# The first stage of an inverse transform, four steps at once on TensorE tiles of 32 by 64, in a kernel of one spectral and two token layers

## Chip, cores and metric

The kernel runs on one core of a Trainium2 chip. The metric is the device time of one execution in microseconds (us), as the median of three runs. Traces come from one profiled execution.

## What is computed

The input `x` is 8 batches of 3072 rows of 256 columns in f32. A spectral layer is followed by two token layers, which see all 24576 rows. Only the first is touched by the change:

```python
X = np.fft.rfft(x, axis=1)
Yr = Xr @ w_r - Xi @ w_i + b_r
Yi = Xr @ w_i + Xi @ w_r + b_i
Yr = np.sign(Yr) * np.maximum(np.abs(Yr) - lam, 0.0)      # Yi alike, lam = 0.01
y = np.fft.irfft(Yr + 1j * Yi, n=3072, axis=1)
# then per token: h = y @ w_in; (h - tanh(h)) @ w_out; soft mixture of 8 experts
```

## The kernel before

The work is a spectral phase and a token phase. Both are written as generators: a step of the one is issued, then pieces of the other where `TOKENS_BESIDE` (line 44) says so. Each engine takes its instructions in the order in which they are written out; there is no planner in the spectral phase.

The transform of 3072 points is split in two stages of small matrices each way. The forward first stage (`f1_piece`, eight pieces a batch, matmuls at line 253) multiplies by `c1` on tiles of 48 rows and 64 columns, two row groups and two column groups, and goes through DRAM (`ad`) to change the layout. Then a batch is worked off in 12 steps of one pair of frequency groups each (`NP` = 12, loop at line 564, 96 steps and 12 more to drain):

- `f2_pair`: eight matmul instructions (line 289) for the second forward stage, evicted by ScalarE (298, 300) and split in a high and a low part (VectorE 301 and 312, `split_sum` on ScalarE 319 and GpSimd 320);
- `mix_part` for the pair before (line 330): `pa` (6 instructions) and `pmix` (12; 18 for the last pair of a batch), 256 columns each; `add_bias` (VectorE 360) reads `pa` from its one PSUM bank, `shrink` (371, 372) adds `pmix`, clips to plus and minus `LAM`, and subtracts the clipped part (380): four pieces of 64 partitions, two on VectorE and two on GpSimd, which also bring the data into the layout that i1 wants;
- `i1_pair` for the pair before that (line 387): one f32 matmul with a 128 x 128 table and 512 columns, which the trace shows as two passes, evicted by ScalarE (389); its store to DRAM (`vd`) is issued at the start of the next step (`flush`);
- `i2_half` (line 415): the second stage of the inverse for the batch before, 16 halves a batch. In the steady state steps 5 to 7 of a batch and steps 0 to 4 of the next take one each, steps 8 to 11 two each. For the last two batches it is two a step; for the last one of all they stand alone after step 96 + 3. ScalarE evicts to `yt` (422; for the last batch 422 and 426), which is stored to `yd`, where the token phase reads it;
- `f1_piece` of the next batch in steps 0 to 7, one each;
- narrowing of f64 weights that the token phase needs, nine small VectorE instructions (lines 496 to 502) per block of 256 columns, one block every three steps, loaded as `raw` one step ahead of use; folding of some of them on TensorE (465, 478).

PSUM has eight banks. Before, `psl` has two for i2 (`i2`, one of them shared with f1) and one for i1; `ps` has two for `pmix`, one each for f1, `f2` and `pa`. The token phase takes over five of them when the spectral steps are over (`ctx.close` at step 96), and the rest later.

All loads and stores named here are issued from SyncE's queue (SP), in the order of the code: flushed stores, then loads of `x` and `v`, stores of `yd`, loads of `a2` and at last `raw`.

In the token phase the lines to know are 748 (plain matmuls of the first chunk), 831 (GpSimd's subtraction of 128 x 512), 894 (logits, `logit_mm`, on four tiles of 128 rows and 32 columns) and 657 (`low_y`).

Of the kernel before, what the change touches and what calls it, by code (L numbers as in the profile page):

```python
# [43 lines left out]
TOKENS_BESIDE = {-4: 1, -2: 1, 0: 1, 1: 2, 2: 3, 3: 4}  # L44


def dft_tables():
# [71 lines left out]
    for j in range(16):  # L119
# [7 lines left out]
    i2[95, : N2 * N1] = (2.0 / S) * np.cos(np.pi * (nn // 32))  # L127
    return {
        "c1": c1.reshape(128, 64).astype(np.float32),
        "f2": f2.reshape(128, NG * 128).astype(np.float32),  # L130
        "i1": i1.reshape(128, 256).astype(np.float32),
        "i2": i2.astype(np.float32),
# [3 lines left out]
def spectral_phase(tc, nb, x, w_r, w_i, b_r, b_i, tb, yd, w_in, w_out, phi, ident, wo32, wh, wl, wp, ew):  # L136

    nc = tc.nc
    with ExitStack() as late, ExitStack() as mid, ExitStack() as ctx:
# [12 lines left out]
        ps = ctx.enter_context(tc.tile_pool(name="fps", bufs=2, space=PSUM))  # L152
# [55 lines left out]
        def load_mix():  # L208
            for w in (w_r, w_i):
                t = thp.tile([128, 512], F32, tag="sw", name="wst", bufs=3)  # L210
# [29 lines left out]
        def f1_piece(b, i):  # L240
            if b == 0 and i < 6:
                asb = stage[i // 3][:, 2 * (i % 3):2 * (i % 3) + 2]
            else:
                asb = ew.gp.tile([128, 2, 512], F32, tag=f"g{3 + i % 2}", name="asb")
            x = xt.pop((b, i))
            tags = ("i2", "f1") if b else (("mix", "f1"), ("mix", "f2"))[i % 2]
            p = [
                psl.tile([128, 512], F32, tag=t, name="pf1") if t == "i2" else
                ps.tile([128, 512], F32, tag=t, name="pf1", bufs=2 if t == "mix" else 1) for t in tags
            ]  # L250
            for c in range(2):
# [5 lines left out]
            for r in range(2):  # L257
                if b == 0 and r == 1 and i not in ACT_F1:
                    nc.vector.tensor_copy(asb[:, r], p[r])
                else:  # L260
                    nc.scalar.activation(asb[:, r], p[r], AF.Copy)
# [70 lines left out]
        def mix_part(b, i, r):  # L332
# [34 lines left out]
        def shrink(b, i):  # L367
# [6 lines left out]
            v = sh[b, i] = thp.tile([128, 2, 256], F32, tag="sw", name="sw", bufs=3)  # L374
            for gg in range(2):
                q = slice(64 * gg, 64 * gg + 64)
                for ri in (1 - gg, gg):
                    e = slice(256 * ri, 256 * ri + 256)
                    eng = nc.gpsimd if ri == gg else nc.vector
                    eng.tensor_tensor(out=v[64 * ri:64 * ri + 64, gg], in0=t[q, e], in1=c[q, e], op=ALU.subtract)  # L380

        def i1_pair(b, i):
            t = sh.pop((b, i)).rearrange("p g e -> p (g e)")
            p = psl.tile([128, 512], F32, tag="i1", name="pi1", bufs=1)
            last = i == NP - 1
# [6 lines left out]
            stores.append((vd[b].rearrange("(g k) (n d) -> (k n) g d", k=4, n=N2)[:, 2 * i:2 * i + 2, :], vs))  # L392
# [125 lines left out]
        if True:  # L518
            load_f2(0, 2)
            for i in range(8):  # L520
                f1_piece(0, i)
# [12 lines left out]
            load_x(1, 2)  # L534
# [3 lines left out]
            for k in range(1, nb):  # L538
                for j in range(8):
                    pieces_at[NP * (k - 1) + j] = (k, j)  # L540

            def piece(t):
                return [pieces_at[t]] if t in pieces_at else []
# [20 lines left out]
            for s in range(T + NP):  # L564
# [15 lines left out]
                if not due:  # L580
                    for j in piece(s):
                        f1_piece(*j)
# [7 lines left out]
                if due:  # L590
                    for j in piece(s):
                        f1_piece(*j)
# [10 lines left out]
                if 2 <= s <= T + 1:  # L603
                    i1_pair(*divmod(s - 2, NP))
# [17 lines left out]
def token_phase(tc, nch, yd, wh, wl, wp, ident, ew):  # L622
# [9 lines left out]
    with ExitStack() as ctx:  # L632
# [21 lines left out]
        def low_y(c):  # L654
            hi, t = ys[c]
            eng = nc.vector if c == 1 else nc.gpsimd
# [60 lines left out]
        def bank(owner=None):  # L717
# [8 lines left out]
            return (ps if k < 4 else ps2).tile([128, 512], F32, tag=f"b{k}", name="ph")  # L726
# [160 lines left out]
        def logit_mm(c, p):  # L887

            if p == 0:
                lp[c] = ps.tile([128, 512], F32, tag="l", name="pl", bufs=1)  # L890
# [143 lines left out]
        ps2 = None  # L1034
# [511 lines left out]
```

## Time and profile before

| | before |
|---|---|
| median of 3 runs | 2079.85 us |
| lowest, highest | 2078.04, 2084.21 us |
| the profiled execution's own time | 2082.89 us |
| span of its trace | 2081.1 us |
| TensorE busy | 1985.7 us (95%) |
| VectorE busy | 1816.1 us (87%) |
| ScalarE busy | 1315.9 us (63%) |
| GpSimd busy | 1348.7 us (65%) |
| granted TensorE clock, mean | 0.980 |

The busy time of TensorE is modelled, since its matmuls are pipelined; durations of single matmuls therefore overlap, and their spacing tells more than their length. The spectral phase fills the first third of the span. Within it, times are best read by batch, that is from the first `f2_pair` matmul of one batch to that of the next, and within a batch by the chain of waits, which lists what followed what on the engine that was late.

### The profile page before, as it was taken

The page shows a single profiled execution, that of the slowest core. Times are in us where ns is not written, and L with a number is a line of the kernel's source. Part 1 is how long each engine was busy: PE and PEld are TensorE (multiplying, and loading weights), DVE is VectorE, ACT ScalarE, POOL GpSimd, SP SyncE. Part 2 cuts the span into 40 slices and gives each one's busy share as a digit, 9 for nine tenths or more (in the row PEclk, how much of TensorE's full clock was granted, in tenths as well). Part 3 has the DMA queues.
Part 4 walks back from the last instruction along what each step waited for, and adds up shares of the span by engine and source line. Part 5 has one row for each costly group of instructions (what it writes and reads, how often), then busy time and mean ns, then how long its engine had stood idle before and what let it go on. Part 6 is the DMA issues. An engine that isn't in the chain of part 4 may idle for free.

```text
span 2081.1 us, 51288 instructions
## 1 busy us (share of the span) xinstructions
PE 1985.7 (95%) x19214; PEld 1683.4 (81%) x19214; DVE 1816.1 (87%) x3555; ACT 1315.9 (63%) x2528; POOL 1348.7 (65%) x1214
## 2 busy tenths in 40 slices
PE   4899999999999999999999999999999999999875
PEld 2678878877887888888888888888888888888633
DVE  3999889999997799999999999999999999999645
ACT  2456666666555666666767666667666676676424
POOL 0444434444442988888888888888888888888300
PEclk7999999999999999999999999999999999999996
DMA  9788898898665677777777777777777777777899
GB/s 268 231 249 262 273 303 261 275 287 268 222 211 182 151 179 175 176 182 175 180 184 178 176 184 173 181 177 180 179 176 181 178 178 183 178 176 183 250 370 385
DMA packets 250550, 445.46 MB, mean 214 GB/s; under 512 B 36160, under 2 KB 144448, under 8 KB 250048
## 3 DMA queue, kind: packets, MB, share of 16 engines
q1 hardware_dynamic: 249264, 440.59, 77.8%
q8 instruction: 153, 2.51, 0.5%
q10 hardware_dynamic: 1040, 1.61, 0.2%
q14 instruction: 93, 0.76, 0.1%
HBM read 139.01 MB, written 105.91 MB: 118 GB/s over the span
## 4 chain that ended last, share of the span: by engine, by line
PE 78%; DVE 12%; DMA 6%; issue 2%; ACT 1%; SPq 1%; POOL 0%; DVEq 0%; ACTq 0%
PE ph L778 45%; PE pl L894 8%; PE pd L1014 8%; PE pmix L330 3%; PE pi L415 3%; DVE sw L380 3%; PE pf L289 2%; PE pi L387 2%; PE pa L330 2%; PE pf L253 2%; DVE t L371 2%; DVE xml L301 1%; DVE t L360 1%; DMA out_dram<-gq 1%; PE ph L748 1%
## 5 line engine op out<-in xcount | busy, mean ns | idle before, releaser
L831 POOL TENSOR_TENSOR g<-g,tanh 128x512 f32<-128x512 f32 x558 | 710.0, 1300 | 159.5 <-ACT tanh L819 159.4
L843 DVE STREAM_TRANSPOSE gt<-g 128x512 f32<-128x512 f32 x752 | 479.1, 680 | 0.5 <-POOL wl L708 0.3
L789 ACT ACTIVATE g<-ph 128x512 f32<-128x512 f32 x564 | 333.1, 591 | 226.8 <-PE ph L778 217.8
L778 PE MATMUL ph<-th,s 128*128 128x256 f32 x2256 | 456.5, 285 | 0.7 <-ACT g L789 0.7
L804 DVE TENSOR_TENSOR g<-ph,g 128x512 f32<-128x512 f32 x564 | 372.8, 681 | 69.0 <-ACT g L789 35.1
L819 ACT ACTIVATE tanh<-g 128x512 f32<-128x512 f32 x564 | 336.9, 621 | 102.6 <-DVE g L804 66.0
L778 PEld LDWEIGHTS ph<-th,s 128*128 128x128 f32 x2256 | 369.9, 191 | 20.2 <-issue 19.4
L778 PE MATMUL ph<-tl,s 128*128 128x256 f32 x1128 | 318.8, 283 | 0.0
L778 PE MATMUL ph<-yh,wl 128*128 128x256 f32 x1128 | 315.9, 280 | 0.0
L778 PE MATMUL ph<-yh,wh 128*128 128x256 f32 x1128 | 315.2, 279 | 0.0
L778 PE MATMUL ph<-y,wh 128*128 128x256 f32 x1128 | 315.1, 279 | 0.0
L380 POOL TENSOR_TENSOR sw<-t,c 64x256 f32<-64x256 f32 x192 | 169.9, 885 | 165.4 <-DVE c L372 121.7
L778 PEld LDWEIGHTS ph<-tl,s 128*128 128x128 f32 x1128 | 215.1, 191 | 0.0
L778 PEld LDWEIGHTS ph<-yh,wh 128*128 128x128 f32 x1128 | 212.9, 189 | 0.1
L778 PEld LDWEIGHTS ph<-y,wh 128*128 128x128 f32 x1128 | 212.1, 188 | 0.0
L778 PEld LDWEIGHTS ph<-yh,wl 128*128 128x128 f32 x1128 | 212.0, 188 | 0.0
L320 POOL TENSOR_TENSOR xml<-xmf,xmh 128x256 fp32r<-128x256 f32 x96 | 74.7, 778 | 206.4 <-issue 144.0
L894 PE MATMUL pl<-g,wp 128*32 128x256 f32 x3072 | 184.8, 381 | 0.0
L1014 PE MATMUL pd<-gq,et 128*32 128x256 f32 x3008 | 170.9, 379 | 0.0
L675 POOL TENSOR_TENSOR tl<-tr,th 128x512 fp32r<-128x512 f32 x94 | 122.0, 1298 | 50.9 <-ACT th L674 30.6
L319 ACT ACTIVATE xmh<-xmf 128x256 fp32r<-128x256 f32 x96 | 40.1, 417 | 181.0 <-DVE xmf L312 164.3
L1014 PEld LDWEIGHTS pd<-gq,et 128*32 128x32 f32 x3008 | 97.8, 110 | 64.5
(206 smaller groups left out, 4450.7 us busy)
## 6 DMA issues: line engine op xcount, KB each, us to landing
gq<-gt SPq DMA_DIRECT2D x1504, 128.0 KB, 2.3
xt<-in_x SPq DMA_DIRECT2D x64, 448.0 KB, 5.4
vd<-vs SPq DMA_DIRECT2D x96, 256.0 KB, 3.6
v<-vd SPq DMA_DIRECT2D x64, 384.0 KB, 5.3
yd<-yt SPq DMA_DIRECT2D x48, 512.0 KB, 5.5
y<-yd SPq DMA_DIRECT2D x48, 512.0 KB, 3.5
a<-ad SPq DMA_DIRECT2D x47, 512.0 KB, 6.2
ad<-asb SPq DMA_DIRECT2D x114, 192.0 KB, 4.3
```

Of the source, the lines that this page charges most:

```text
L320: nc.gpsimd.tensor_tensor(out=lo[:, 0], in0=sm, in1=hi[:, 0].bitcast(F32), op=ALU.subtract)
L330: nc.tensor.matmul(o, st[u], w[m], start=first and k == 0, stop=last and k == 2)
L380: eng.tensor_tensor(out=v[64 * ri:64 * ri + 64, gg], in0=t[q, e], in1=c[q, e], op=ALU.subtract)
L675: nc.gpsimd.tensor_tensor(out=lo, in0=t, in1=hi.bitcast(F32), op=ALU.subtract)
L778: nc.tensor.matmul(o[:, 256 * j:256 * j + 256], a[u][:, 128 * j:128 * j + 128], y[v], start=new and j == 0 and k == 0, stop=n in (2, 3, 4) ...
L789: nc.scalar.activation(e[n], o.rearrange("p (j n) -> p j n", j=2), AF.Copy)
L804: nc.vector.tensor_tensor(out=h, in0=o, in1=h, op=ALU.add)
L819: nc.scalar.activation(t, g, AF.Tanh)
L831: eng.tensor_tensor(out=g, in0=g, in1=th.pop((c, w, n)), op=ALU.subtract)
L843: nc.vector.transpose(out=t[:, :, :, 2 * (p % 4) + u, :], in_=g[:, u, :].rearrange("p (q k i) -> p q k i", q=4, k=4))
L894: nc.tensor.matmul(lp[c][q:q + 32, 0:256], wp[:, 2 * p + f, :], half_of(c, gs[c, p + f // 2][:, f % 2], h), start=p == 0 and f < 2, stop=p ...
L1014: nc.tensor.matmul(o[32 * a:32 * a + 32, f], ex[c][:, k, :], g[a][:, k], start=k == 0, stop=k == 3)
```

## The change

- `i1_pair` becomes `i1_four`: in every fourth step (1, 5 and 9 of a batch) four pairs are transformed at once. Instead of one matmul of 128 rows and 128 columns a pair, there are 32 matmuls of 32 rows, 64 columns and 256 moving elements, on all four row groups and both halves of the columns, each row group with a PSUM bank of its own. Two evictions of 128 x 1024 take the place of four of 128 x 512, and two stores of 512 KB that of four of 256 KB.
- The table `i1` is turned for it, and the rows of `i2` are permuted, since the order of the rows in `vd` is another. Both tables are inputs.
- `shrink` subtracts once, 128 x 512, on GpSimd; VectorE's two subtractions go. `sw` has five buffers instead of three, `t` two instead of one.
- Four banks (`psm`, tags `x0` and `x1`, two banks each) serve i1 and f1 by turns. f1's pieces of later batches move to the end of a step and stand in pairs, in steps 0, 2, 4 and 6 of the batch before (2, 2, 3, 4, 4, 6, 6, 7 for the second batch), each evicted by one ScalarE instruction instead of two.
- i2 and `pmix` have one bank each instead of two.
- The token phase reads and splits its first block at steps 86 and 89 instead of 92 and 94, and subtracts its low part on VectorE. It starts with three banks instead of four and opens four more at its third position, when `psm` is closed.

```diff
-TOKENS_BESIDE = {-4: 1, -2: 1, 0: 1, 1: 2, 2: 3, 3: 4}
+TOKENS_BESIDE = {-10: 1, -7: 1, 0: 1, 1: 2, 2: 3, 3: 4}
...
-        psl = late.enter_context(tc.tile_pool(name="fpl", bufs=2, space=PSUM, side="right"))
+        psl = late.enter_context(tc.tile_pool(name="fpl", bufs=1, space=PSUM, side="right"))
...
+        psm = mid.enter_context(tc.tile_pool(name="fpm", bufs=1, space=PSUM, side="right"))
...
-        ps = ctx.enter_context(tc.tile_pool(name="fps", bufs=2, space=PSUM))
+        ps = ctx.enter_context(tc.tile_pool(name="fps", bufs=1, space=PSUM))
...
+        def stage_banks(k):
+            return psm.tile([128, 2, 512], F32, tag=f"x{k}", name="px")
+
-        def f1_piece(b, i):
+        def f1_piece(b, i, k):
...
-            tags = ("i2", "f1") if b else (("mix", "f1"), ("mix", "f2"))[i % 2]
-            p = [
-                psl.tile([128, 512], F32, tag=t, name="pf1") if t == "i2" else
-                ps.tile([128, 512], F32, tag=t, name="pf1", bufs=2 if t == "mix" else 1) for t in tags
-            ]
+            p = stage_banks(k)
             for c in range(2):
                 for r in range(2):
                     nc.tensor.matmul(
-                        p[r][64 * c:64 * c + 64], c1[64 * r:64 * r + M1], x[64 * r:64 * r + M1, 512 * c:512 * c + 512],
+                        p[64 * c:64 * c + 64, r], c1[64 * r:64 * r + M1], x[64 * r:64 * r + M1, 512 * c:512 * c + 512],
                         start=True, stop=True,
                     )
...
+            if b:
+                nc.scalar.activation(asb, p, AF.Copy)
...
-                    pm[b, i] = ps.tile([128, 512], F32, tag="mix", name="pmix", bufs=2)
+                    pm[b, i] = ps.tile([128, 512], F32, tag="mix", name="pmix")
...
-            t = half[b, i] = thp.tile([128, 512], F32, tag="t", name="t", bufs=1)
+            t = half[b, i] = thp.tile([128, 512], F32, tag="t", name="t", bufs=2)
...
-            v = sh[b, i] = thp.tile([128, 2, 256], F32, tag="sw", name="sw", bufs=3)
-            for gg in range(2):
-                q = slice(64 * gg, 64 * gg + 64)
-                for ri in (1 - gg, gg):
-                    e = slice(256 * ri, 256 * ri + 256)
-                    eng = nc.gpsimd if ri == gg else nc.vector
-                    eng.tensor_tensor(out=v[64 * ri:64 * ri + 64, gg], in0=t[q, e], in1=c[q, e], op=ALU.subtract)
-
-        def i1_pair(b, i):
-            t = sh.pop((b, i)).rearrange("p g e -> p (g e)")
-            p = psl.tile([128, 512], F32, tag="i1", name="pi1", bufs=1)
-            last = i == NP - 1
-            for v, s in (((0, slice(0, 256)), (1, slice(256, 512))) if last else ((0, slice(0, 512)),)):
-                nc.tensor.matmul(p[:, s], i1[:, 128 * v:128 * v + 128], t[:, s], start=True, stop=True)
-            vs = vp.tile([128, 2, 256], F32, tag="v", name="vs")
-            nc.scalar.activation(vs, p, AF.Copy)
+            v = sh[b, i] = thp.tile([128, 512], F32, tag="sw", name="sw", bufs=5)
+            nc.gpsimd.tensor_tensor(out=v, in0=t, in1=c, op=ALU.subtract)
+
+        def i1_four(b, i):
+            t = [sh.pop((b, 4 * i + c)) for c in range(4)]
+            p = [stage_banks(k) for k in range(2)]
+            for h in range(2):
+                for ri in range(2):
+                    for r in range(4):
+                        q = slice(32 * r, 32 * r + 32)
+                        for c in range(2):
+                            k = 64 * ri + 128 * (4 * i + 2 * h + c == NP - 1 and r >= 2)
+                            nc.tensor.matmul(
+                                p[r // 2][64 * c:64 * c + 64, r % 2, 256 * h:256 * h + 256], i1[q, k:k + 64],
+                                t[2 * h + c][q, 256 * ri:256 * ri + 256], start=ri == 0, stop=ri == 1,
+                            )
...
+            dst = vd[b].rearrange("(i r h a) (n d) -> i (a n) (r h) d", h=2, a=4, r=4, n=N2)[i]
+            for k in range(2):
+                vs = vp.tile([128, 4, 256], F32, tag="v", name="vs")
+                nc.scalar.activation(vs.rearrange("p a n -> p (a n)"), p[k].rearrange("p r n -> p (r n)"), AF.Copy)
+                stores.append((dst[:, 4 * k:4 * k + 4], vs))
...
-                for j in range(8):
-                    pieces_at[NP * (k - 1) + j] = (k, j)
+                for j, t in enumerate((2, 2, 3, 4, 4, 6, 6, 7) if k == 1 else (0, 0, 2, 2, 4, 4, 6, 6)):
+                    pieces_at.setdefault(NP * (k - 1) + t, []).append((k, j))
...
-                if 2 <= s <= T + 1:
-                    i1_pair(*divmod(s - 2, NP))
+                if s % 4 == 1 and 5 <= s <= T + 1:
+                    i1_four(*divmod((s - 5) // 4, NP // 4))
+                for k, j in enumerate(piece(s)):
+                    f1_piece(*j, k)
...
-            eng = nc.vector if c == 1 else nc.gpsimd
+            eng = nc.gpsimd if c > 1 else nc.vector
...
-                k = next(banks) % (4 if ps2 is None else 6)
+                k = next(banks) % (3 if ps1 is None else 6)
...
             if s == 3:
                 ew.open_mid()
+                ps1 = pool("tps1", 1, space=PSUM)
```

## Rows read from the trace of the kernel before

**Rows 1.** The page: shares of the chain that ended last, by engine.
```profile
PE 78%; DVE 12%; DMA 6%; issue 2%; ACT 1%; SPq 1%; POOL 0%; DVEq 0%; ACTq 0%
```

**Rows 2.** Windows by batch: us, busy by engine (instructions), PEclk, DMA share, GB/s.
```profile
54.53:107.82 53.29, 45.59 (x313) 34.92 (x312) 50.69 (x92) 25.21 (x52) 22.74 (x27) 1.00 0.74 228
...
256.81:331.82 75.01, 74.88 (x561) 61.67 (x560) 66.53 (x130) 48.57 (x89) 30.56 (x36) 1.00 0.89 280
...
479.78:554.72 74.94, 73.41 (x537) 59.16 (x536) 70.66 (x130) 45.36 (x84) 33.88 (x40) 1.00 0.85 265
554.72:622.57 67.85, 63.62 (x470) 56.55 (x469) 64.49 (x120) 37.64 (x66) 31.34 (x36) 1.00 0.65 208
...
652.23:669.64 17.41, 16.33 (x130) 14.80 (x128) 16.36 (x35) 14.41 (x33) 2.71 (x2) 1.00 0.56 182
```

**Rows 3.** Chain of waits from 318 us: start, us, what.
```profile
322.10 0.71 PE pa L330 x6
322.82 1.44 PE pmix L330 x12
324.25 0.89 PE pi L415 x8
325.14 0.86 PE pi L387 x2
326.01 0.89 PE pf L289 x8
...
334.25 1.02 PE pf L253 x8
335.27 0.91 PE pa L330 x6
```

**Rows 4.** Chain of waits from 625 us, where batches end and tokens start.
```profile
652.92 1.05 ACT yh L651
...
654.78 1.17 PE pi L415 x8
655.97 0.75 ACT yt L422
656.73 0.12 ACT yt L426
656.89 1.17 PE pi L415 x8
...
672.71 1.86 PE pl L894 x32
```

**Rows 5.** Timeline of VectorE over three steps: start, us, line, operation.
```profile
600.52 0.69 DVE L371 TENSOR_TENSOR t<-t,pmix 128x512 f32<-128x512 f32 x1
...
618.48 0.69 DVE L371 TENSOR_TENSOR t<-t,pmix 128x512 f32<-128x512 f32 x1
...
619.67 1.29 DVE L380 TENSOR_TENSOR sw<-t,c 64x256 f32<-64x256 f32 x2
```

**Rows 6.** Groups by line: busy us, mean ns of one | idle before, releaser.
```profile
L831 POOL TENSOR_TENSOR g<-g,tanh 128x512 f32<-128x512 f32 x558 | 710.0, 1300 | 159.5 <-ACT tanh L819 159.4
...
L422 ACT ACTIVATE yt<-pi 128x384 f32<-128x384 f32 x90 | 79.7, 885 | 10.3 <-PE pi L415 10.1
...
L253 PEld LDWEIGHTS pf<-xt,c 48*64 48x64 f32 x384 | 10.3, 131 | 6.0 <-issue 0.8 <-ACT yt L422 0.5 <-ACT asb L261 0.3
```

**Rows 7.** Timelines of GpSimd and VectorE at the eighth batch's end.
```profile
626.76 2.78 POOL L657 TENSOR_TENSOR y<-y,yh 128x1024 fp32r<-128x1024 f32 x1
...
627.26 2.31 DVE L306 COPY d<-xmf 128x2 f32<-128x2 f32 x1
```

**Rows 8.** The page: DMA issues, KB each, median us to landing.
```profile
vd<-vs SPq DMA_DIRECT2D x96, 256.0 KB, 3.6
v<-vd SPq DMA_DIRECT2D x64, 384.0 KB, 5.3
```

**Rows 9.** VectorE's waits from 107 to 555 us: total us, times, longest.
```profile
DVE da L496 <- DMA raw<-in_moe_w_in: 2.3, 3, 1.5
```

More of the change, by code (lines that the diff above doesn't have):

```diff
@@ L127, in dft_tables @@
     i2[95, : N2 * N1] = (2.0 / S) * np.cos(np.pi * (nn // 32))
+    turned = np.zeros((128, 2, 2, 64))
+    for gg in range(2):
+        for q in range(2):
+            for v in range(2):
+                for ri in range(2):
+                    turned[64 * gg + 32 * q:64 * gg + 32 * q + 32, v, ri] = i1[cols(ri, q), v, 64 * q:64 * q + 64]
+    kap = np.arange(96).reshape(3, 2, 2, 4, 2).transpose(0, 3, 1, 2, 4).reshape(-1)
     return {
@@ L130, in dft_tables @@
         "f2": f2.reshape(128, NG * 128).astype(np.float32),
-        "i1": i1.reshape(128, 256).astype(np.float32),
-        "i2": i2.astype(np.float32),
+        "i1": turned.reshape(128, 256).astype(np.float32),
+        "i2": i2[kap].astype(np.float32),
     }
@@ L209, in load_mix @@
             for w in (w_r, w_i):
-                t = thp.tile([128, 512], F32, tag="sw", name="wst", bufs=3)
+                t = thp.tile([128, 512], F32, tag="sw", name="wst", bufs=5)
                 nc.sync.dma_start(
@@ L253, in f1_piece @@
                     nc.tensor.matmul(
-                        p[r][64 * c:64 * c + 64], c1[64 * r:64 * r + M1], x[64 * r:64 * r + M1, 512 * c:512 * c + 512],
+                        p[64 * c:64 * c + 64, r], c1[64 * r:64 * r + M1], x[64 * r:64 * r + M1, 512 * c:512 * c + 512],
                         start=True, stop=True,
                     )
[L257 to L261, printed above, removed]
+            if b:
+                nc.scalar.activation(asb, p, AF.Copy)
+            else:
+                for r in range(2):
+                    if r == 1 and i not in ACT_F1:
+                        nc.vector.tensor_copy(asb[:, r], p[:, r])
+                    else:
+                        nc.scalar.activation(asb[:, r], p[:, r], AF.Copy)
             if i == 0:
@@ new lines, in shrink @@
+            nc.gpsimd.tensor_tensor(out=v, in0=t, in1=c, op=ALU.subtract)
[3 more added lines that the diff above has]
+            for h in range(2):
+                for ri in range(2):
+                    for r in range(4):
[6 more added lines that the diff above has]
+                            )
@@ L390, in i1_pair @@
             if i == 0:
                 vd[b] = dram.tile([96, N2 * D], F32, tag="vd", name="vd", bufs=2)
-            stores.append((vd[b].rearrange("(g k) (n d) -> (k n) g d", k=4, n=N2)[:, 2 * i:2 * i + 2, :], vs))
+            dst = vd[b].rearrange("(i r h a) (n d) -> i (a n) (r h) d", h=2, a=4, r=4, n=N2)[i]
[3 more added lines that the diff above has]
+                stores.append((dst[:, 4 * k:4 * k + 4], vs))
@@ L520, in spectral_phase @@
             for i in range(8):
-                f1_piece(0, i)
+                f1_piece(0, i, i % 2)
             load_mix()
@@ L538, in spectral_phase @@
             for k in range(1, nb):
-                for j in range(8):
-                    pieces_at[NP * (k - 1) + j] = (k, j)
+                for j, t in enumerate((2, 2, 3, 4, 4, 6, 6, 7) if k == 1 else (0, 0, 2, 2, 4, 4, 6, 6)):
+                    pieces_at.setdefault(NP * (k - 1) + t, []).append((k, j))
             def piece(t):
-                return [pieces_at[t]] if t in pieces_at else []
+                return pieces_at.get(t, [])
             i2_at, v2_at, y_steps = {}, {}, {}
@@ L579, in spectral_phase @@
                     i2_half(*j)
-                if not due:
-                    for j in piece(s):
-                        f1_piece(*j)
                 for j in due_w.get(s - 5, ()):
@@ L589, in spectral_phase @@
                 pump(3)
-                if due:
-                    for j in piece(s):
-                        f1_piece(*j)
                 if m:
@@ L722, in bank @@
             else:
-                k = next(banks) % (4 if ps2 is None else 6)
+                k = next(banks) % (3 if ps1 is None else 6)
             if owner:
                 holds[owner] = k
-            return (ps if k < 4 else ps2).tile([128, 512], F32, tag=f"b{k}", name="ph")
+            return (ps if k < 3 else ps1).tile([128, 512], F32, tag=f"b{k}", name="ph")
         homes = chain(
@@ L889, in logit_mm @@
             if p == 0:
-                lp[c] = ps.tile([128, 512], F32, tag="l", name="pl", bufs=1)
+                lp[c] = ps1.tile([128, 512], F32, tag="l", name="pl", bufs=1)
             for f in range(4):
@@ L1033, in token_phase @@
         ps = pool("tps", 1, space=PSUM)
-        ps2 = None
+        ps1 = None
         done = set()
```

1 line of the change is left out of this document (removed).

## The prediction

> **What bounds the kernel now.** I read the chain that ended last first: TensorE holds 78% of the span and VectorE 12% [rows 1]. That is an average over two halves. The change touches only the spectral half (0 to some 670 us); the token half runs the same instructions on the same number of PSUM banks, so I leave its time alone. So I cut the spectral half at the starts of its 12-step batches and read each stretch [rows 2]. From the second batch to the seventh (107.82 to 554.72 us, 72 steps, 446.9 us, 6.21 us a step) TensorE shows 98 to 100% busy at granted clock 1.00 and VectorE 89 to 94%; VectorE has some ten instructions a step with about 0.05 us between two, so it has next to nothing left either. In the first batch VectorE is at 95% and TensorE at 86%. DMA stands at 0.85 to 0.89 in mid-phase. So TensorE and VectorE are both at their limits, and relief of one alone would soon meet the other.
>
> The chain of waits inside a step gives TensorE's bill [rows 3]: second forward stage 0.89, one half of the inverse's second stage 0.89, mixing 0.71 + 1.44, the inverse's first stage (i1) 0.86. A piece of the first forward stage (f1) takes 1.02, and the mixing right behind it 0.91 where it is 0.71 without: 1.22 with its surroundings, of which 0.86 is streaming (i1 streams the same 512 columns of f32 in two passes in 0.86); 0.36 goes into changing over to small tiles and back.
>
> Twelve steps: 12 x (0.89 + 2.15 + 0.86) + 8 x 1.22 + 16 x 0.89 + 0.72 (six more mixing matmuls at 0.12 for the last pair) = 71.5 us. Six batches, less the five halves that the second batch doesn't have yet (4.5), make 424.7 of the 446.9 us; the other 22 are folding of weights and waits.
>
> **The change, part by part.**
> *i1 on TensorE.* Four steps cost 4 x 0.86 = 3.44 us. After: 32 f32 matmuls of 256 columns, two passes each, 64 instructions on eight tiles of 32 x 64. The before kernel has no such tile. The nearest row is the logit matmul: 32 instructions of 256 columns, four tiles side by side, 1.86 us [rows 4], that is 0.23 a round of four. If eight run side by side, 64 instructions are again eight rounds: 1.86, plus the 0.20 that the next full-size matmul loses [rows 3], 2.06. If only four do, 3.72 + 0.20 = 3.9. f1 already runs tiles on two row groups and two column groups at once, 8 instructions in 1.02, so both directions overlap; I take 2.06. Gain 1.38 x 24 groups = 33 us (bounds: a loss of 11 to a gain of 38 with no change-over).
> *f1 in pairs.* 27 pairs pay one change-over instead of two: 27 x 0.36 = 10 us gained. Its two evictions become one of 1024 elements, 1.05 us [rows 4].
> *Shrinkage.* VectorE loses two 64-partition subtractions, 1.29 us a step [rows 5]; GpSimd's two become one of 128 x 512, 1.30 us [rows 6]. Starts of the same VectorE line three steps apart lie 17.96 us apart (600.52, 618.48) [rows 5]; without the subtractions it would be 14.1. Some comes back: while GpSimd runs its `low_y`, 2.78 us, a copy of two elements on VectorE takes 2.31 [rows 7], so a VectorE instruction behind the new 1.30 us can be held. I charge 0.45 a step (0 to 1.3): 15.4 per three steps, 5.1 a step against 5.98 now. TensorE after the change: 71.5 - 3 x 1.38 - 4 x 0.36 = 65.9, 5.5 a step. TensorE stays the longer one, on average only: steps without f1 and i1 take 0.89 + 0.89 + 2.15 = 3.93 (two a batch), the others up to 6.9. In a 3.93 step VectorE can fall 1.2 behind, and the next `pa` matmul waits for `add_bias` to free its one bank: 0 to 2.4 us a batch, I take 0.7, 4 us in six batches.
> *One bank for the inverse's second stage (i2) and for mix instead of two.* From the end of one half to the next: 0.28 until ScalarE starts (1.17 - 0.89), 0.89 eviction [rows 6], 0.04 back, 1.2 us. Where 0.89 of second forward stage lies between two halves (steps 8 to 9, 10 to 11, 11 to 12 of a batch, and six in the eighth), 0.31 is missing; where mixing lies between, it is hidden, except that after an i1 group ScalarE has two evictions of 1.05 first. 24 x 0.31 + 6 x 0.4 = 10 us (0 to 20). Mix: its reader is done some 3 us before the next writer; nothing.
> *The tail of i2.* The sixteen halves of the last batch run alone, 652.23 to 669.64 us, 17.4 us [rows 2]. The chain there: 1.17 TensorE, 0.75 + 0.12 ScalarE, then the next TensorE piece after 2.11 us [rows 4]; with two banks two halves share such a round. With one bank each half pays it: 16 x 2.11 = 33.8. **A loss of 16.4 us**, with nothing else on TensorE's queue to cover it.
> *Stores and loads on SyncE.* `vd` goes out 1 MB every four steps; packets and bytes stay. Behind the last store wait the last batch's `v` loads; median landings are 3.6 and 5.3 us [rows 8], and a four times larger store ends later: 0 to 3, I take 1.5. Four `ad` stores and two `x` loads now stand together on SP's queue ahead of the weight load `raw`, which VectorE needs one step later. Now it waits 2.3 us in three places, at most 1.5 [rows 9]; 24 loads in the six batches, bounds 0 and 24 x 1.5 = 36; I take 9, since half of them follow a burst and VectorE has gained slack.
> *Token start moved.* `low_y(0)` leaves GpSimd at step 94, where it delayed the last pair (2.31 for a tiny copy, TensorE idle behind it): 3 us gained; on VectorE six steps earlier it is covered by slack of 0.4 a step. Three instead of four banks for the first plain chunks: a bank is held some 3 us of the 4.2 that three take; nothing.
>
> **The sum.** Second to seventh batch: gain 18 x 1.38 + 24 x 0.36 = 33.5, waits of today partly gone (10 of the 22), against 4 + 8 + 9 = 21 of new ones: -22. First batch, bound by VectorE (53.3 us for nine steps, 5.9 each): to 5.1 it is -7. Eighth: two groups and VectorE's relief -6, `low_y` -3, one bank +2: -7. Tail +16.4 + 1.5. Together -18. The profiled execution took 2082.9 (span 2081.1), so 2064.9; the median of the runs lies 3.0 lower, 2079.85: forecast **2062 us**.
>
> **A rule that speaks against it.** The logit matmuls' loads of weights, on the same 128 rows, follow at 0.23 a round without standing out [rows 4]. The Trainium skill, TensorE: Matmul & The Clock Gate, Part 3: Packing small matmuls, says that a weight load overlaps running matmuls only where its row group differs. By that rule each of the eight rounds here, which use all four row groups, would show its load; what that gives is the third rival. The trace so far speaks against the rule.
>
> **The rivals.**
> 1. *The waits eat it.* Steps settle at some 6.0: VectorE's heavy steps fall on TensorE's short ones, `raw` lands late in most steps, ScalarE's order delays i2. The gains of the three stretches shrink to 10, 4 and 4, the tail stays: 2079.85 - 18 + 18, about 2080. For it: VectorE at 89 to 95% [rows 2], DMA at 0.89. Against: VectorE's 1.29 a step really goes.
> 2. *Slower: only four of the eight tiles run together.* Place: the i1 group, 3.9 us for 3.44. Then 24 x 1.84 = 44 us of the forecast's gain are missing, but longer steps hide some 15 of the new waits: about 2062 + 29 = 2091. It turns slower than before once a group takes over 3.0 us. Against it: f1's four tiles and the logits' four, both at full overlap.
> 3. *Loads stand out.* Eight rounds of 0.23 + 0.13 (a 64-column load takes 131 ns [rows 6]) + 0.20 = 3.1 us a group, 25 us less gained, of which some 10 are hidden by fewer waits: about 2077.
> 4. *Better.* The new waits are covered and the other 12 of today's go too: -18 - 21 - 12 = -51, about 2029.
>
> **How the numbers follow.** Forecast 0.60 (own range 2046 to 2073), rival 1 0.18, rival 2 0.08, rival 3 0.05, rival 4 0.09. About 0.3% (6 us) is what a measurement of this kernel can tell from no change. Faster: forecast, rival 4 and a little of 1: 0.70. Same: most of rivals 1 and 3: 0.18. Slower: rival 2 and the upper end of 1: 0.12. The range reaches from between rival 4 and the forecast to the upper part of rival 1: 2040 to 2086.
>
> **What would show it.** Right: 64 i1 instructions in about 2.1 us, 24 times; mean step of batches two to seven 5.9; the sixteen last i2 halves about 34 us; VectorE under 85% in mid-phase; first batch near 5.1 a step. Wrong: an i1 group over 3 us; TensorE idle ahead of `pa` behind VectorE or of i2 behind ScalarE by more than 25 us in all; a tail under 25 us, which would mean that the one bank isn't what I take it for.

## The result, and the profile after

The changed kernel takes 2109.69 us (median; 2105.41 to 2110.65) against 2080.83 us for the kernel before in the same runs: a ratio of 1.0134 [1.0113, 1.0155]. It is slower by some 29 us, where 2062 us was forecast. The profiled execution took 2110.65 us, its span is 2108.9.

The windows by batch, cut as in [rows 2] at the first `f2_pair` matmul of a batch (the first line from step 3 on, as there) and at the first and last of the sixteen halves that end i2. Columns: stretch, us, busy us (instructions) of TensorE, weight loads, VectorE, ScalarE, GpSimd, then granted clock, DMA share, GB/s. The two lines of the tail are one stretch, cut where the clock has changed.

```profile
46.49:104.73 58.24, 44.81 (x435) 36.38 (x431) 40.17 (x73) 26.77 (x45) 18.40 (x18) 0.91 0.79 228
...
104.73:558.99 454.26, 424.11 (x4248) 365.83 (x4249) 330.88 (x637) 277.47 (x428) 160.10 (x156) 0.97 0.89 267
...
558.99:627.23 68.24, 62.09 (x639) 57.50 (x637) 55.91 (x95) 40.82 (x63) 25.75 (x26) 0.97 0.67 210
...
652.34:664.00 11.66, 6.35 (x42) 5.29 (x40) 11.13 (x21) 5.76 (x12) 2.70 (x2) 0.90 0.42 106
664.00:696.03 32.03, 22.50 (x89) 19.55 (x89) 5.21 (x15) 8.60 (x20) 0.00 (x0) 0.50 0.22 74
```

Against [rows 2] this gives a ledger of spans. The column e1 is the best of the versions tried below.

| stretch | before | after | difference | forecast | e1 |
|---|---|---|---|---|---|
| start to step 12 | 107.8 | 104.7 | -3.1 | -7 | 105.2 |
| steps 12 to 83 (72 steps) | 446.9 | 454.3 | **+7.4** | -22 | 410.8 |
| step 84 to the first tail half | 97.5 | 93.4 | -4.2 | -7 | 90.8 |
| the sixteen tail halves | 17.4 | 43.7 | **+26.3** | +17.9 | 17.0 |
| the rest, tokens | 1411.5 | 1412.9 | +1.4 | 0 | 1410.0 |

So the tail is nearly the whole of the loss, and the 72 steps, which were to pay for it, gave nothing. Two things stand out in the second line. VectorE fell from 412.75 us busy to 330.88, 73%, as intended. But TensorE, which stood at 98% before, now sits idle for 30 us and runs at a mean clock of 0.97 instead of 1.00: six times, for some 24 us in all, the granted clock is 0.50, that is 1.2 GHz, and each of these stretches begins in, or at most 1.4 us behind, a wait of `pa` of 1.6 to 3.0 us.

What it waits for is in the lists of waits of the changed kernel between 104 and 560 us (engine, instruction, what released it: total us, times, longest). First TensorE's longest, then VectorE's, then SyncE's queue:

```profile
PE pa L340 <- DVE t L370: 19.7, 14, 3.0
```
```profile
DVE xml L311 <- ACT xmh L310: 60.6, 38, 2.8
DVE da L510 <- DMA raw<-in_moe_w_out: 21.4, 11, 2.9
DVE da L510 <- DMA raw<-in_moe_w_in: 19.7, 9, 3.9
```
```profile
SPq L172 <- ACT vs L405: 97.4, 34, 13.3
SPq L172 <- ACT asb L265: 92.4, 24, 13.2
```

VectorE now waits 41 us for the weight loads, where [rows 9] had 2.3 for those from `in_moe_w_in` (and 0.4 for the others). In the kernel before, SyncE's queue stood like this between 107 and 555 us:

```profile
SPq L164 <- ACT vs L389: 151.2, 62, 5.4
SPq L164 <- ACT asb L261: 40.2, 22, 3.1
```

In all it stood as long as now, 191 and 190 us; but then for 5.4 us at most and now for up to 13.3 at a time. The chain of waits from 262 us shows one late load from end to end (start, us, what):

```profile
262.42 1.06 PE px L260 x8
...
264.42 1.01 ACT asb L265
...
266.46 0.67 SPq L172
...
267.18 0.62 SPq L189
...
268.35 0.45 SPq L445
...
268.90 8.77 DMA raw<-in_moe_w_out
277.67 0.02 issue
277.69 0.29 DVE da L510
...
278.65 0.61 DVE t L370
```

A pair of f1 pieces is multiplied at the end of its step. Its second eviction ends at 265.4. SyncE has meanwhile stood before the flush of the next step; now it issues four `ad` stores (L172), two `x` loads (L189), a `yd` store, and only then, at 268.90, the weight load. The load lands at 277.7, when VectorE has already been waiting for 2.9 us. Behind `da` on VectorE's queue stands `add_bias` (L370), which TensorE's next `pa` needs. In this step TensorE still had other work and didn't stand. At 391 us it did (timelines of VectorE and TensorE: start, us, line, what, idle before and its releaser):

```profile
390.17 0.29 DVE L510 TENSOR_SCALAR da<-raw 128x256 int32<-128x256 int32 x1 [3.93 <-DMA raw<-in_moe_w_in]
```
```profile
391.78 0.50 PE L340 MATMUL pa<-wah,xmh 128*128 128x256 f32 x1 [3.00 <-DVE t L370]
```

Ten of the fourteen waits of `pa` for L370, 14.1 of the 19.7 us, follow such a wait of VectorE for its weights.

### The profile page after: what moved, and what is told of

It is laid out like the page before. It is cut to its first block, busy times and chain, and to the rows that moved or that the text cites. A ratio compares the mean times of both kernels' runs of the same rounds, so it can differ in the third digit from the quotient of the medians.

```text
span 2108.9 us, 53323 instructions
## 1 busy us (share of the span) xinstructions
PE 1978.8 (94%) x20542; PEld 1702.7 (81%) x20542; DVE 1707.7 (81%) x3364; ACT 1315.8 (62%) x2424; POOL 1300.9 (62%) x1117
## 4 chain that ended last, share of the span: by engine, by line
PE 72%; DMA 12%; DVE 6%; issue 4%; ACT 3%; SPq 2%; POOL 0%; ACTq 0%; DVEq 0%; POOLq 0%
PE ph L787 44%; PE pl L903 8%; PE pd L1023 8%; PE pmix L340 4%; DMA raw<-in_moe_w_in 3%; DMA raw<-in_moe_w_out 2%; PE pa L340 2%; PE px L396 2%; PE pi L429 2%; DVE xml L311 1%; DMA ewt<-in_moe_w 1%; PE px L260 1%; DMA out_dram<-gq 1%; PE pf L299 1%; DVE t L370 1%
## 5 line engine op out<-in xcount | busy, mean ns | idle before, releaser
L385 POOL TENSOR_TENSOR sw<-t,c 128x512 f32<-128x512 f32 x96 | 130.8, 1362 | 217.6 <-DVE c L382 203.8
L429 PE MATMUL pi<-i,v 96*128 96x128 f32 x1024 | 151.3, 294 | 20.6 <-ACT yt L440 14.8
L311 DVE TENSOR_TENSOR xml<-xmf,xmh 128x512 fp32r<-128x512 f32 x96 | 106.8, 1112 | 77.1 <-ACT xmh L310 76.6
L429 PEld LDWEIGHTS pi<-i,v 96*128 96x128 f32 x1024 | 134.5, 204 | 30.6 <-ACT yt L440 18.9
```

What stands on the lines that cost most here:

```text
L311: nc.vector.tensor_tensor(out=lo[:, 1:3], in0=p, in1=hi[:, 1:3].bitcast(F32), op=ALU.subtract)
L385: nc.gpsimd.tensor_tensor(out=v, in0=t, in1=c, op=ALU.subtract)
L429: nc.tensor.matmul(p[:, a, :], t[:, 4 * u + a, :], i2[:, 96 * n2:96 * n2 + 128], start=True, stop=True)
```

## The experiments

The edits are short, and most kernels are the changed kernel plus named edits: **spare bank**, **weights first**, **two buffers**, **early pairs**, **x first**, **vector shrink**. "72 steps" is the stretch from step 12 to step 84 in the profiled run.

| run | edits | median us | ratio to before | 72 steps | tail |
|---|---|---|---|---|---|
| after | none | 2109.7 | 1.0134 [1.0113, 1.0155] | 454.3 | 43.7 |
| a1 | spare bank | 2078.1 | 0.9989 [0.9974, 1.0004] | 444.5 | 17.1 |
| a5 | idle work in the tail | 2091.9 | 1.0059 [1.0040, 1.0078] | 450.6 | 34.0 |
| a2 | weights first | 2098.8 | 1.0093 [1.0078, 1.0108] | 436.2 | 45.7 |
| a3 | early pairs | 2088.7 | 1.0044 [1.0029, 1.0059] | 435.6 | 45.1 |
| a6 | spare bank, weights first | 2068.5 | 0.9951 [0.9934, 0.9968] | 438.0 | 17.1 |
| c1 | a6 + two buffers | 2054.4 | 0.9871 [0.9857, 0.9886] | 431.0 | 17.1 |
| c2 | c1 + x first | 2051.2 | 0.9859 [0.9837, 0.9880] | 424.2 | 17.1 |
| c3 | c1 + early pairs | 2043.9 | 0.9825 [0.9806, 0.9843] | 418.8 | 17.1 |
| c4 | c1 + vector shrink | 2047.2 | 0.9839 [0.9818, 0.9859] | 425.9 | 17.1 |
| g1 | c1 + early pairs, vector shrink | 2042.6 | 0.9826 [0.9810, 0.9842] | 417.9 | 17.1 |
| e2 | c1 + early pairs, x first | 2046.2 | 0.9836 [0.9821, 0.9851] | 412.6 | 17.1 |
| e1 | all six | 2036.9 | 0.9798 [0.9776, 0.9820] | 410.8 | 17.0 |
| h1 | e1, x first from step 12 on | 2036.1 | 0.9785 [0.9765, 0.9804] | 410.8 | 17.1 |
| e3 | e1 without spare bank | 2068.4 | 0.9948 [0.9933, 0.9963] | 410.8 | 45.7 |
| b1 | kernel before, weights first | 2080.3 | 1.0005 [0.9994, 1.0016] | 445.8 | 17.4 |

The column of the 72 steps comes from one profile each. After, a1 and a5 issue the same instructions there and differ by up to 10 us, at mean clocks of 0.97, 0.99 and 0.98; so, where the clock falls, only larger steps, or those that the medians repeat, are read as effects. At clock 1.00 the column repeats far better: e1, e3 and h1, again with the same instructions, agree to 0.02 us.

**The tail: a bank, then the clock (a1, a5).** a1 opens a bank after step T + 3, when the pool of i1 closes, and gives it to every second half:

```diff
-            p = psl.tile([128, 4, 128], F32, tag="i2", name="pi2")
+            p = (psx[0] if psx and u else psl).tile([128, 4, 128], F32, tag="i2", name="pi2")
...
                 if s == T + 3:
                     mid.close()
+                    psx.append(late.enter_context(tc.tile_pool(name="fpx", bufs=1, space=PSUM, side="right")))
...
-                lp[c] = ps1.tile([128, 512], F32, tag="l", name="pl", bufs=1)
+                lp[c] = ps2.tile([128, 512], F32, tag="l", name="pl", bufs=1)
```

> The changed kernel, with one more bank for every second half of the inverse's second stage in the drain behind step 99 only; the logit bank moves to a later pool for it. Theory one (the tail is lost to the single bank, and the clock falls because TensorE then idles 0.95 us in every round): the sixteen last halves fall from 43.7 to about 17.5 us at granted clock 1.00, and the whole from about 2110 to 2084 us. Rival (the tail would be slow anyway, since the loads of v come late or the clock was low already from the waits ahead of it): the halves stay above 25 us and the whole above 2092. The 72 steps in mid-phase stay at about 454 us under both.

a5 keeps the one bank and lets TensorE multiply into that spare bank while it would be idle; nothing reads those results, so the kernel only does more work than it needs.

```diff
+            if psx:
+                o = psx[0].tile([128, 4, 128], F32, tag="idle", name="pidle")
+                for a in range(4):
+                    nc.tensor.matmul(o[:, a, :], t[:, a, :], i2[:, 0:128], start=True, stop=True)
```

> The changed kernel with its single bank for the last halves, plus four idle matmuls behind each of the last sixteen halves, written to a spare bank that nobody reads. It parts the tail's loss in two. If the clock fell because TensorE idles, the granted clock stays at 1.00, and the sixteen halves take 16 x 2.1 = 34 us instead of 43.7, the whole about 2100. If the clock falls for another reason, the halves stay at 43 us or grow.

TensorE's timeline in the changed kernel's tail (start, us, line, what, idle before and its releaser):

```profile
656.99 1.16 PE L429 MATMUL pi<-i,v 96*128 96x128 f32 x8 [0.95 <-ACT yt L440]
659.11 1.16 PE L429 MATMUL pi<-i,v 96*128 96x128 f32 x8 [0.96 <-ACT yt L440]
661.22 1.80 PE L429 MATMUL pi<-i,v 96*128 96x128 f32 x8 [0.96 <-ACT yt L440]
663.98 2.08 PE L429 MATMUL pi<-i,v 96*128 96x128 f32 x8 [0.95 <-ACT yt L440]
667.01 2.08 PE L429 MATMUL pi<-i,v 96*128 96x128 f32 x8 [0.95 <-ACT yt L440]
```

The first rounds are 2.11 us long, as forecast from [rows 4]. Then the same eight matmuls take 2.08 instead of 1.16, at a granted clock of 0.50, that is 1.2 GHz, and a round takes 3.03. Between them TensorE does nothing for 0.95 us in each round. In a5 TensorE is busy for 32.48 of 34.05 us, the clock stays, and the stretch takes what the forecast gave it without the fall, 16 x 2.11 = 33.8. The windows of the tail in a5 and in a1:

```profile
647.53:681.58 34.05, 32.48 (x258) 29.62 (x256) 16.35 (x35) 15.08 (x34) 2.71 (x2) 1.00 0.34 105
```
```profile
642.00:659.10 17.10, 16.15 (x129) 14.81 (x128) 16.35 (x35) 14.13 (x32) 2.71 (x2) 1.00 0.66 205
```

So of 26.3 us lost in the tail some 10 are the clock and some 17 the bank. The clock is also still at 0.50 when the tokens start, which costs another 1.5 us there:

```profile
696.03:699.10 3.07, 3.07 (x9) 2.46 (x9) 0.00 (x0) 1.00 (x3) 0.00 (x0) 0.50 0.34 133
```

a1 gains 31.6 in the median, 6 more than expected; tail and start of the tokens explain 28.1 of it. e3 (below) says 31.5 for the same edit, of which its windows show 28.7 in the tail. a5 gains 17.8, 8 more than expected; the same two places explain 11.2. What is left, 1 to 7 us, is not located.

**The weight load's place (a2, b1).** `load_w` moves from the end of a step to its beginning, ahead of the flush, by itself:

```diff
                 b, i = divmod(s, NP)
+                for j in due_w.get(s, ()):
+                    load_w(j)
                 flush()
...
-                for j in due_w.get(s, ()):
-                    load_w(j)
```

> The changed kernel, with the weight load raw issued at the start of its step, ahead of the flushed stores, instead of at the end. Theory one (raw stands behind stores that wait for the late evictions of the pair of first-stage pieces, so that SyncE issues it 4 to 5 us late): VectorE's waits for raw fall from some 50 us to under 10, and the whole by 12 to 25 us, to about 2090. Rival one (bursts on the DMA engines make it late, whatever the order): waits stay above 25 us, the whole within 5 us of 2110. Rival two (VectorE's waits for raw are covered, and what counts is ScalarE's order): waits go, the whole stays within 5 us.

b1 is the same edit in the kernel before.

> The kernel before, with raw issued at the start of its step in the same way. A control: if the late raw comes from the change, nothing is to be had here, 2080 within 4 us; if before had lost to it as well, 5 us or more are gained.

In b1 the time doesn't move, so the place is a matter of the change alone. In a2 VectorE's wait for weights falls from 41 us to 0.9, and the time by 10.9 us, less than expected. SyncE's queue shows why, from 105 to 541 us:

```profile
SPq L457 <- DVE dl L516: 135.9, 24, 11.3
```

The load (L457) has one buffer, which VectorE's last narrowing operation (L516) frees late. Earlier in the queue, it stands there itself, 136 us in all, and holds up the flush, `x`, `v` and `a2` behind it. The stall moved. That a queue stands is no loss by itself: in b1 it stands 132 us behind the same load, and the kernel takes as long as before.

**Two buffers (c1, a6).** c1 is a1 and a2 with the weights in two buffers by turns. a6 is c1 without the second buffer.

```diff
-            raw = dcp.tile([128, 256, 2], I32, tag="raw", name="raw", bufs=1)
+            raw = dcp.tile([128, 256, 2], I32, tag="raw", name="raw", bufs=2)
```

> a1 and a2 together: spare bank in the tail, weight loads at the head of the step into their one buffer. Theory (the tail and the queue are separate losses, and the one buffer's share is what c1 has beyond it): 2109.7 less 31.6 less 10.9 = 2067, 13 us above c1. Rival (a1's tail also moved the 72 steps, so the two overlap): 2072 or more.

> The changed kernel with the spare bank in the tail (as in a1) and the weight loads at the head of SyncE's queue in a step (as in a2), now into two buffers by turns, so that such a load never waits for the narrowing before it. Theory (in a2 the one buffer only moved the stall: SyncE's queue stood 136 us behind loads that waited for their buffer, and the x and v loads behind them came late): the stretch of 72 steps falls from a2's 436 us to some 428, time about 2057. Rival (what a2 left is VectorE beside GpSimd and ScalarE's order, SyncE's blocked queue cost nothing): the stretch stays at 436, time about 2066 (a1's 2078 less a2's 11). If both waits were the same loss: about 2070.

a6 comes out within 2 us of what a1 and a2 add up to, so the tail and the queue are separate losses. The second buffer gives another 14.1 us. So mending the weights' way brings 10.9 + 14.1 = 25 us, more than half of it only seen once the first part is mended. Two buffers with the load left at its old place were not run.

**The place of the f1 pairs (a3, c3).** The pair goes back to where single pieces stood in the kernel before, ahead of the folding and the mixing of its step.

```diff
+                for k, j in enumerate(piece(s)):
+                    f1_piece(*j, k)
                 for j in due_w.get(s - 5, ()):
                     fold_w(j)
...
-                for k, j in enumerate(piece(s)):
-                    f1_piece(*j, k)
```

> The changed kernel with one edit: the pairs of the first forward stage ahead of folding and mixing. Theory (what c3 gained is the place of the pairs in ScalarE's and SyncE's queues, and it is there in the change as it stands): 10 us better than the change, about 2099, the weight loads waiting less behind the flushed stores (L172 <- ACT asb falls). Rival (the waits for the weights hide it): within 4 us of the change.

> As c1, with the pairs of the first forward stage back ahead of the folding and the mixing of their step, where they stood in the kernel before. Theory (their two evictions of 0.96 us stand in ScalarE's queue ahead of the next step's xmf and hold up the mixing there): 4 to 8 us better than c1, the long step 0 of a batch shorter by 1 us. Rival (the pair then delays pa, and with it VectorE's chain): 0 to 6 us worse than c1.

Alone it gives 21.0 us, twice what was expected; on top of c1 10.6. The two overlap: with the pair early, the flushed stores are ready sooner, and SyncE reaches the weight load sooner. In a3 the same stretch of the queue's waits reads

```profile
SPq L172 <- ACT asb L265: 31.2, 12, 4.6
```

against 92.4 us in the change, and VectorE's wait for weights falls from 41 to 25 us (12.9 and 12.0). What c3 still gains where no weight load waits fits the other effect: the pair's evictions no longer stand on ScalarE ahead of the next step's `xmf`. In c1 ScalarE waits 19.8 us for the pairs' matmuls with `xmf` behind it, in c3 0.7, and VectorE's wait for `xmh` (L310) falls from 78.2 to 68.0. The flush waits less for `asb` too (84.7 to 37.6); no run parts the two.

**x ahead of the stores (c2).**

```diff
+                for j in piece(s + 3):
+                    load_x(*j)
                 flush()
...
-                for j in piece(s + 3):
-                    load_x(*j)
```

> As c1, and the x loads too are issued ahead of the stores that a step flushes. Theory (any load behind a store that waits for ScalarE comes late): 3 to 6 us better than c1, x landing near 5.2 us again. Rival (x is loaded three steps ahead, so its lateness is covered): within 2 us of c1.

3.2 us in the median, 2051.19 (2048.14 to 2054.48) against 2054.43 (2052.21 to 2054.8): at the edge of what can be told. From issue to landing `x` takes no less time by the median, 8.1 us against 7.2 in c1. In the 72 steps the edit gives nearly the same wherever it is made: 6.8 us from c1 to c2, 6.1 from c3 to e2, 7.1 from g1 to e1. The medians gain 3.2, -2.4 and 5.7, since step 12 begins later with the edit each time, by 3.5, 10.2 and 1.2 us; whether that is the edit's doing is not settled (see g1 and h1).

**The subtraction on VectorE again (c4, e2).**

```diff
-            nc.gpsimd.tensor_tensor(out=v, in0=t, in1=c, op=ALU.subtract)
+            nc.vector.tensor_tensor(out=v, in0=t, in1=c, op=ALU.subtract)
```

> As c1, with the shrinkage's subtraction of 128x512 on VectorE instead of GpSimd. Theory (GpSimd's 1.36 us operation slows the VectorE operation beside it, L311, from 0.77 to 1.13, and that stretches the short steps): L311 near 0.77 again, VectorE pays 0.68 for the subtraction and gets 0.36 back, near 5.4 us a step in all: within 4 us of c1. Rival (VectorE is the bound of the stretch again): slower than c1 by 10 to 25 us.

VectorE has more to do, 344.3 us in the 72 steps against c1's 327.9, and the kernel is faster by 7.2 us, where no gain was expected. The groups by line (busy us, mean ns | idle before), first of c1, then of c4:

```profile
L311 DVE TENSOR_TENSOR xml<-xmf,xmh 128x512 fp32r<-128x512 f32 x72 | 78.1, 1084 | 78.5 <-ACT xmh L310 78.2
```
```profile
L385 DVE TENSOR_TENSOR sw<-t,c 128x512 f32<-128x512 f32 x72 | 49.9, 693 | 2.5
L311 DVE TENSOR_TENSOR xml<-xmf,xmh 128x512 fp32r<-128x512 f32 x72 | 49.6, 689 | 61.8 <-ACT xmh L310 61.8
```

How one engine holds up the other is seen in the changed kernel's timelines of GpSimd and VectorE at 334 us (start, us, line, what):

```profile
334.63 1.29 POOL L385 TENSOR_TENSOR sw<-t,c 128x512 f32<-128x512 f32 x1 [2.29 <-DVE c L382]
```
```profile
334.67 1.80 DVE L311 TENSOR_TENSOR xml<-xmf,xmh 128x512 fp32r<-128x512 f32 x1
```

L311 reads two operands from SBUF; it starts 0.04 us behind GpSimd's subtraction and takes 1.80 us, not far from what is left of GpSimd's 1.29 plus its own 0.69, 1.94. L381, with one operand in PSUM, keeps its 0.69 beside GpSimd, as at 251 us:

```profile
251.15 0.73 POOL L330 TENSOR_TENSOR xml<-xmf,xmh 128x256 fp32r<-128x256 f32 x1 [1.59 <-issue]
```
```profile
251.28 0.69 DVE L381 TENSOR_TENSOR t<-t,pmix 128x512 f32<-128x512 f32 x1
```

The Trainium skill, SBUF — State Buffer, section "SBUF: two separate sides", says that VectorE operations with two SBUF inputs and GpSimd operations share a pair of ports under an exclusive lock, so that the second waits out the first; the 1.80 us at 334 us agrees. The kernel before waited in the same way: of its two subtractions on VectorE, 1.29 us together, the one that starts behind GpSimd's takes 0.86 us and the other 0.42, while in c4 VectorE does the whole subtraction in 0.69.

> As e1, but with the subtraction on GpSimd as the change has it. If the two engines beside each other still cost what c4 showed: 5 to 7 us slower than e1, some 2040. If TensorE is the bound by then: within 2 us of e1.

e2, with the subtraction on GpSimd, is 9.3 us slower than e1: 1.8 of it in the 72 steps and 6.2 before step 12 (111.3 against 105.2). g1 is c3 with the same edit, and gains 1.2 us in the median and 0.8 in the 72 steps. So c4's gain (5.2 in the 72 steps) is not repeated once the pairs are early: with TensorE the bound, the place of the subtraction is worth 1 to 2 us there, and the 6.2 before step 12 are not explained.

**All together, and the price of the tail (e1, e3).**

> All edits together: spare bank in the tail, weight loads and x loads at the head of the step with two buffers for the weights, the pairs of the first forward stage early, the shrinkage's subtraction on VectorE. Theory (the losses lie at different places, so they add): c1's 2054 less 3 (loads) less 10.5 (early pairs) less 7 (subtraction) = 2033, the 72 steps near 406 us. Rival (they hide one another, TensorE being the bound after the first two): no better than c3's 2044.

> As e1, but with the tail on its one bank as the change has it. Theory (the tail stands alone, so its price doesn't hang on what goes before): 32 us slower than e1 by a1, of which 16.7 the rounds of 2.11 us and some 10 the fall of the clock; about 2065. Rival (a part of a1's 32 us came from the 72 steps, 454 against 444 us, and not from the tail): 24 to 27 us slower than e1.

e1 is the best version but for h1, which can't be told from it: 43 us faster than the kernel before, 73 faster than the change, and 3.5 slower than if the single gains had added up. Its 72 steps, in windows, and a piece of its chain of waits from 400 us:

```profile
105.16:515.97 410.81, 407.89 (x4249) 354.80 (x4249) 339.05 (x706) 274.88 (x428) 63.47 (x84) 1.00 0.96 296
```
```profile
400.64 0.89 PE pf L299 x8
401.54 0.89 PE pi L430 x8
402.43 0.71 PE pa L340 x6
403.14 1.44 PE pmix L340 x12
404.58 0.89 PE pf L299 x8
405.48 0.89 PE pi L430 x8
406.37 1.88 PE px L260 x16
408.25 0.90 PE pa L340 x6
```

TensorE is busy for 407.9 of 410.8 us, at full clock, and the chain is TensorE alone. With the same 4249 matmul instructions the changed kernel shows 424.1 us of busy time and 30 us idle: of the 43 us between the two 16 are busy time and 27 are waits. Of the 16 the clock can be no more than 12, half of the 24 us at 0.50. Most of the other 4 is there at full clock too where the pairs come late, as in c2 (its window follows); e2 is c2 with early pairs, and there TensorE is busy for 408.6 us, also at clock 1.00.

```profile
105.17:529.37 424.20, 411.98 (x4249) 356.16 (x4249) 327.10 (x635) 277.19 (x427) 160.84 (x156) 1.00 0.93 286
```

So an idle TensorE is paid for twice, as a wait and by the clock. e3 puts the one-bank tail back: 31.5 us slower, the whole of a1's gain, and the 72 steps stay at 410.8. The rival, that part of a1's gain came from the 72 steps, falls.

**The first batch (g1, h1).** Step 12 began at 99.6 to 111.3 us in the experiments, and e1 and c2 lay on the late side.

> As e1, but with the x loads behind the flushed stores again, as the change has them. Theory (x ahead of the stores delays the first batch, where the second forward stage waits for the stores of the first: step 12 began at 105.2 in e1 and c2 against 99.6 to 101.6 in c1, c3 and c4): 4 to 5 us better than e1, about 2032. Rival (these differences of step 12 come and go from run to run): within 2 us of e1's 2037.

> As e1, but in the first twelve steps the x loads stay behind the flushed stores and only from step 12 on go ahead of them. Theory (ahead of the stores they help the 72 steps, 410.8 against g1's 417.9, and cost the first batch up to 4 us, since the second forward stage waits there for those stores): some 2033. Rival (the first batch swings from run to run for another reason, its weight load and the half clock at 50 to 76 us, whatever the x loads do): within 2 us of e1's 2037.

g1 is 5.7 us slower than e1, not faster, and loses it in the 72 steps (417.9 against 410.8). h1, with the old order in the first batch only, is within 1 us of e1. Step 12 begins at 103.9 us in g1, 104.4 in h1, 105.2 in e1 and, with the same instructions up to there as e1, 107.8 in e3. Such differences come without any edit, and the order of the loads isn't shown to move the first batch. What the trace of the change shows there is a weight load of 12.5 us that ends at 54.1 us, and a mean clock of 0.65 between 46.5 and 60.0 us, with 0.97 from there to 72.0. Why the first batch's length differs between kernels stays open.

## Why the prediction was wrong, point by point

Three steps failed: the weight load (9 us charged, 25 to be had by mending it), the place of the f1 pairs (nothing charged, 10.6 to 21), and the clock of an idle TensorE (nothing charged, some 10 in the tail and up to 12 in the 72 steps). They overlap.

- **i1 in eight tiles: right.** Of the 24 groups 23 take 1.91 to 1.93 us, and one at 572 us, partly at clock 0.50, takes 2.39; 0.20 is lost behind a group. That is 2.13 against 2.06 in all:

```profile
319.40 1.93 PE px L396 x64
```

  That is 24 x (3.44 - 1.93 - 0.20) = 31 us off TensorE, where 33 were forecast. Rivals 2 (only four tiles at once) and 3 (loads stand out), and with it the rule that the prediction held against itself, fall with this row: eight rounds take 0.24 each. The sign came out as in rival 2, but not by its mechanism.
- **f1 in pairs: right on TensorE, and its main cost missed.** Two single pieces took 2 x 1.22; a pair takes 1.88, and the mixing behind it 0.90 instead of 0.71 (rows of e1 above): 0.37 saved, where 0.36 was forecast. But the step priced only the change-over and the length of the eviction. It didn't ask who stands behind the two evictions: ScalarE's next `xmf`, and SyncE's flush with everything in its queue. Early pairs gave back 21 us alone and 10.6 beside c1.
- **TensorE's bill: right, 5.5 forecast.** The last two batches of e1's 72 steps take 67.3 us each, 5.61 a step. Thus the gain in the 72 steps was there to be had, with the six edits: 446.9 - 410.8 = 36, more than the 22 forecast.
- **The weight load: failed, 9 us for 25.** The row was read, the queue was named and the bounds (0 to 36) were right, but 9 was taken, because half of the loads follow a burst and VectorE had slack. VectorE waited 41 us, and mending it was worth 25. The slack of VectorE is an average; the load is issued one step before it is needed, and the burst ahead of it now waited for the slowest thing in the step, the late pair. [rows 9] showed lateness while the queue ran with short stalls; the term should have been taken from the new order of events (end of the pair, two evictions, seven issues ahead of it, 5 us of landing, which became 6.2 to 6.6 in the median), which doesn't fit into a step.
- **An idle TensorE loses clock: not in the forecast at all.** At full use [rows 2] shows 1.00 throughout. Every term was priced as time at that clock. It was 0.97 in the 72 steps (at most 12 us) and 0.50 in most of the tail (some 10) and at the start of the tokens (1.5), whose time was to stay as it was.
- **The tail: mechanism right, size off.** 16 x 2.11 held as long as the clock did. 17.9 with the stores became 26.3.
- **One bank for i2 in mid-phase: too dear.** 8 to 10 us were charged; no matmul of `pi` shows a wait for ScalarE in the changed kernel (their weight loads show 4.5 us), in c1 they show 2 us, and e1, still with one bank, has TensorE idle for 2.9 us in the 72 steps over all.
- **VectorE: the sum good enough, the place wrong.** A drop of 1.29 - 0.45 = 0.84 a step was forecast; busy time fell by 1.14, from 5.73 (412.75 / 72) to 4.60 (330.88 / 72), for the kernel before had waited behind GpSimd as well. The interference now hits one operation above all, L311, on which the chain to the mixing hangs.
- **First batch, 5.1 a step forecast: 6.5** (58.24 us for nine). VectorE's waits for weights of 9 us in two places, with half clock in and behind them; the rest is open, as told above.
- **The marks set beforehand.** VectorE under 85% and the i1 group were met; the mean step (6.3 for 5.9), the tail (43.7 for 34) and the first batch were not. The mark for failure, 25 us of TensorE idle behind VectorE or ScalarE, was set on lists that show 19.7 for `pa` and nothing for i2: the loss was there all the same, since TensorE was idle for 30 us over more lines than these two, and the clock took its part where nothing is listed as a wait.

Rival 1 (the waits eat the gain) had the right mechanism and about 2080; it became 2110 with the fall of the clock and the dearer pairs.

## What to carry to other kernels

Where work is bundled, go through every queue that the bundle passes and ask what stands right behind it: here a load needed one step later, behind four stores that wait for the bundle's own evictions. Take such a load's lateness from the new order of events, not from an average slack, and when it is moved ahead, look whether its buffer is free by then. And reckon that an idle TensorE may lose its clock as well: giving up a second bank cost one more round trip for every second tile, and then half of the clock.

## What was not expected of the hardware

In the tail TensorE had gaps of 0.95 us in rounds of 2.11 us, and the granted clock fell to 0.50 after three to four rounds (661 us in the change; in e3 after two) and stayed there for the thirty microseconds that the pattern went on. Filled with useless matmuls, the same rounds kept 1.00. A VectorE operation on two SBUF operands took 1084 ns in the mean with the subtraction on GpSimd and 689 without, single ones 1.80 us, while its neighbours with an operand in PSUM kept 0.69.
